# Attention moved ahead by half a batch, scores of both token halves in one stay, and M's last two quarters made in the batch that uses them

## The chip, the cores and the metric

The kernel runs on one core of a Trainium2 chip. The metric is the device time of one execution in microseconds (us), here the median of three runs. The profile shows one further execution, instruction by instruction, on the five engines: TensorE (PE, with its weight loads as PEld), VectorE (DVE), ScalarE (ACT), GpSimd (POOL) and SyncE (SP), which issues almost all DMAs.

## The reference, cut to what matters

There are 8 batches of 576 tokens and 8 heads of 64. Thirty-two packed queries `p` attend to `k` and `v`; then all tokens `q` attend to the 32 packed rows. The result goes through a two-layer MoE expert with a gate.

```
def sm_attn(qq, kk, vv):
    s = scale * np.matmul(qq, kk.transpose(0, 1, 3, 2))
    s = s - np.max(s, axis=-1, keepdims=True)
    a = np.exp(s)
    a = a / (np.sum(a, axis=-1, keepdims=True) + 1e-09)
    return np.matmul(a, vv)
p_packed = sm_attn(p, k, v)
out = sm_attn(q, p_packed, p_packed)          # B, H, S, D
x = out.transpose(0, 2, 1, 3).reshape(B * S, H * D)
h = x @ w_in                                   # 512 -> 2048
g = h * np.clip(h + 3.0, 0.0, 6.0) / 6.0
return g @ w_out                               # 2048 -> 512
```

## The kernel before

**What is multiplied.** `out @ w_in` is not formed as such. For each batch the kernel makes M = (packed rows) x `w_in` in four column quarters (`u_m`, L528) and multiplies the second attention's probabilities `a` with it. Each fp32 value is split into a high and a low part (`hi`, `lo`), so each product is three fp32r matmuls. The first product of a step, `ps_hh<-a,m` (L929), is six matmuls; the gate follows (ACT L940, then DVE L941), and the second product goes into accumulators `acc` (L969).

**Steps.** From batch 1 on, a batch is two halves of tokens (c = 0 and c = 1), each with 16 steps over the 16 column blocks f of `w_in`. The document counts steps 0 to 31 within a batch as s = 16 c + position. In batch 1, c = 0, every block is a step of `moe` (L1014). All later halves run `moe_pairs` (L1106): twelve steps form six pairs (four pairs in batch 1) whose second product is a seven-product scheme on half tiles with prepared combinations T1, T2, T4 of `w_out` (tiles `wt`), and the last four steps are single. Products go into four PSUM accumulators A, B, C and D; C and D are free between a half's last pair and the next half's first pair, except that in odd batches the edge rows use D at the end of c = 0. A pair's product is issued one to two steps after its blocks were gated.

**Combinations.** `combine(i)` (L1057) makes pair i's combinations in batch 1 at the steps listed in `TURN`: POOL adds (L1071), DVE subtracts (L1082 to L1095), and `kept` (L1073) splits each of four results with an ACT cast (L1075) and a DVE subtraction (L1076). Pairs 0, 1 and 4, 5 share two slots, are stored in DRAM and fetched back by `fetch_t` (L1103) at the steps in `FETCHES`.

**Attention of the next batch** runs in between, a few pieces at each step. `fill` (L1401) advances generators; `STAGES` gives for each the step at which it starts and how many pieces it makes per step. `attention_inputs` (L558) loads `p`, `k` and the first `q` tiles and turns them with DVE transposes (L322, L555); `attention` (L579) holds `u_s1` (scores of the packed queries, maximum, exponential), the turns of `q`, `u_ets` (transposes of the exponentials, L440 and L447), `u_pvs` (product with `v`, L470, scaled on DVE at L474) and `u_ppt` (L480, L482); `u_s2` makes the second scores and `u_a` the probabilities (DVE L502 to L524). A load's buffer, `nat`, exists twice and is shared with the upper `v` rows.

**Stays.** Scores, M and the product with `v` use small tiles of the array (64 x 32 and the like) while all else uses 128 x 128. A run of such small matmuls on PE is called a stay. `both_halves` (L362) makes the scores of the two token halves in one stay or in two; in one stay it needs two more PSUM banks, which `spare_ps` (L325) takes from C and D.

**M's quarters.** `first_quarters` (L1382) fetches three quarters of `w_in` in turn into one buffer (`w_again`, shared with `v_nat`) from s = 21 of the batch before, makes M from each, finishes all three at s = 31 and then fetches the fourth, which `late` makes in the first steps of the batch itself.

**What sets the order.** Each engine runs its instructions in order. Within what the code above allows, a scheduler places them; `behind_gates` (L542) and `issue_after` keep attention work behind the gate of the step before. SP's queue, too, is in order: a load that waits for a buffer holds up all later ones.

Of the kernel before, what the change touches and what calls it, by code (L numbers as in the profile page):

```python
# [19 lines left out]

STAGES = (((0, 1), (6, 2), (19, 2)), ((0, 1), (10, 2), (19, 1)))


LATE = (3, 2, 1, 2, 1)
PAIRS = 6
FIRST_PAIRS = 4
TURN = (
    (5, 5, 6, 6, 7, 7, 7), (7, 8, 8, 9, 9, 9, 10), (10, 10, 11, 11, 12, 12, 12), (13, 13, 13, 14, 14, 15, 15),  # L30
    (27, 27, 28, 28, 28, 29, 29), (29, 29, 30, 30, 30, 31, 31),
)
FETCHES = (((5, 1), (7, 0)), ((5, 4), (7, 5)))

# [41 lines left out]
def packed_attention_moe(  # L78
# [150 lines left out]
                yield  # L229

    def att_ps():
        return spare_ps(0) if steady else ps_a.tile([P, 512], F32, name="ps1", tag="att")

    def att_pair():

# [138 lines left out]
    def u_s1(b):  # L374
        kt = [state.pop(("k", b, a)) for a in range(NPAIR)]
        pt = state.pop(("p", b))
        e = [ap.tile([P, NST * P], F32, name="e", tag="e", bufs=4) for _ in range(2)]
        mx = [sm.tile([P, 2], F32, name="mx") for _ in range(2)]
        for part in both_halves(b == 1, pt, kt):
            if part is None:  # L380
                yield 1
                continue
            hf, banks = part
            for x, s in enumerate(banks):
                nc.scalar.copy(out=e[x][:, hf * HS:(hf + 1) * HS], in_=s)
                yield 1
                nc.vector.reduce_max(out=mx[x][:, hf:hf + 1], in_=s, axis=AX.X)
                yield None if x else 1
        for x in range(2):
            nb = sm.tile([P, 1], F32, name="nb")  # L390
            nc.vector.tensor_scalar(
                out=nb, in0=mx[x][:, 0:1], scalar1=mx[x][:, 1:2], scalar2=-scale, op0=ALU.max, op1=ALU.mult
            )
            yield 1
            den = sm.tile([P, 1], F32, name="den")
            rinv = sm.tile([P, 1], F32, name="rinv")
            state["e", b, x] = (e[x], rinv)
            nc.scalar.activation(
                out=e[x][:, :S], in_=e[x][:, :S], func=AF.Exp, bias=nb, scale=scale, accum_out=den
            )  # L400
            yield
            nc.vector.tensor_scalar_add(den, den, 1e-9)
            yield 1
            nc.vector.reciprocal(rinv, den)
            yield 1
# [79 lines left out]
    def u_s2(b):  # L485
        qt = [state.pop(("q", b, a)) for a in range(NPAIR)]
        z = [ap.tile([P, T, NPK], F32, name="z", tag="e", bufs=4) for _ in range(2)]
        for part in both_halves(not roles, pps[b % 2], qt):
            if part is None:
                yield 1  # L490
                continue
            hf, banks = part
            for x, s in enumerate(banks):
                nc.vector.transpose(out=z[x].rearrange("p t n -> p (t n)")[:, hf * HS:(hf + 1) * HS], in_=s)
                yield None if x else 1
        for x in range(2):
            yield from u_a(b, x, z[x])
# [57 lines left out]
        nc.vector.transpose(out=t, in_=state.pop(("nat", which, b, a)))  # L555
        state[which, b, a] = t

    def attention_inputs(b):  # L558

        load_p(b)  # L560
        load("k", b, 0)
        load("k", b, 1)
        yield
        transpose_p(b)
        turn("k", b, 0)
        load("k", b, 2)
        yield
        turn("k", b, 1)
        load("k", b, 3)
        yield  # L570
        turn("k", b, 2)
        load("q", b, 0)
        yield
        turn("k", b, 3)
        load("q", b, 1)
        load_v_low(b)
        yield

    def attention(b):  # L579

        yield from coarse(u_s1(b))
        turn("q", b, 0)
        load("q", b, 2)
        yield
        turn("q", b, 1)
        load("q", b, 3)
        yield
        yield
        turn("q", b, 2)
        load_v_high(b, 0)  # L590
        yield
        turn("q", b, 3)
        load_v_high(b, 1)
        yield
        yield from coarse(u_ets(b))
        yield from coarse(u_pvs(b))
        yield
        yield from coarse(u_ppt(b))
# [458 lines left out]
    def combine(i):  # L1057

        if i == 0:
            tiles = [wr.tile([P, 4, 2, H2], F32R, name=f"wt{n}", tag=f"w_in{n}") for n in (1, 2, 3)]  # L1060
            for k, name in enumerate(("T1", "T2", "T4")):
                for pair in range(PAIRS):
                    n, at = ((0, k), (1, k), (2, k), ((2, 0, 1)[k], 3))[pair % 4]
                    blocks[pair, name] = [tiles[n][:, at, x] for x in range(2)]
            for n in range(2):
                slots[n] = tiles[n].bitcast(F32)[:, :3]
        x, y = (xp.tile([P, W + P], F32, name="wx", tag="tb")[:, :H2] for _ in range(2))

        def whole(dst, name):
            hi, lo = (z.bitcast(F32) for z in block(i, name))  # L1070
            nc.gpsimd.tensor_tensor(out=dst, in0=hi, in1=lo, op=ALU.add)  # L1071

        def kept(name, made):  # L1073
            hi, lo = block(i, name)
            nc.scalar.copy(out=hi, in_=made)  # L1075
            nc.vector.tensor_sub(out=lo, in0=made, in1=hi.bitcast(F32))  # L1076

        whole(x, "T3")
        yield
        whole(y, "B22")  # L1080
        yield
        nc.vector.tensor_sub(out=y, in0=x, in1=y)  # L1082
        hi, lo = (z.bitcast(F32) for z in block(i, "B11"))
        nc.vector.tensor_sub(out=x, in0=x, in1=hi)
        nc.vector.tensor_sub(out=x, in0=x, in1=lo)
        yield
        kept("T1", x)
        yield
        nc.vector.tensor_sub(out=x, in0=hi, in1=y)
        nc.vector.tensor_add(out=x, in0=x, in1=lo)  # L1090
        kept("T2", x)
        yield
        hi, lo = (z.bitcast(F32) for z in block(i, "B21"))
        nc.vector.tensor_sub(out=x, in0=hi, in1=x)
        nc.vector.tensor_add(out=x, in0=x, in1=lo)  # L1095
        kept("T4", x)
        yield
        kept("T3", y)
        if i % 4 < 2:
            nc.sync.dma_start(out=t_kept[i % 4 + i // 4 * 2], in_=slots[i % 4].rearrange("p a x m -> p (a x m)"))  # L1100
        yield
# [4 lines left out]
    def moe_pairs(b, c, fill):  # L1106

        pairs = list(range(FIRST_PAIRS if b == 1 else PAIRS))
        if c == 0:
            pairs.reverse()  # L1110
        n_pairs = len(pairs)
        steps = [2 * i + k for i in pairs for k in range(2)] + list(range(2 * n_pairs, NF))

# [265 lines left out]
        t = w_in_sb[n] = wr.tile([P, FPC, NPAIR, P], F32, name="w_again", tag="w_in0")  # L1379
        nc.sync.dma_start(out=t.rearrange("p f a e -> p (f a e)"), in_=w_kept[n])  # L1380

    def first_quarters(b):  # L1382

        for n in range(NCH - 2, -1, -1):
            fetch_w_in(n)
            yield
            yield
            yield from coarse(u_m(b, n))

    for b in range(1, B):  # L1390
        more = b + 1 < B
        inputs, packed, ahead = (x(b + 1) if more else iter(()) for x in (attention_inputs, attention, u_s2))
        ahead = coarse(ahead)
        if b == 1:
            late = coarse(part for n in range(1, NCH) for part in u_m(1, n))
            turned = [combine(i) for i in range(PAIRS)]
        else:
            late = coarse(u_m(b, NCH - 1))
        soon = first_quarters(b + 1) if more else iter(())

        def fill(c, f):  # L1401
            s = c * NF + f
            with behind_gates():
                if b == 1:
                    for _ in range(LATE[s] if s < len(LATE) else 0):
                        next(late, None)
                    if s == 0:
                        with tc.issue_after(state["stored"].ins):
                            for n in range(NCH):
                                keep_w_in(n)  # L1410
                    for i in range(PAIRS):
                        for _ in range(TURN[i].count(s)):
                            next(turned[i], None)
                else:
                    if s > 0:
                        next(late, None)
                    for at, i in FETCHES[c]:
                        if f == at:
                            fetch_t(i)
                if s >= 21:  # L1420
                    next(soon, None)
                if s == 31 and more:
                    rest(soon)
                    fetch_w_in(NCH - 1)
            with tc.issue_after(state["load"].ins), behind_gates():
                for chain, (start, count) in zip((inputs, packed, ahead), STAGES[b > 1]):
                    for _ in range(count if s >= start else 0):
                        next(chain, None)

        for c in range(2):  # L1430
# [3 lines left out]
                roles.extend((3, 0, 1, 2))  # L1434
            else:
                moe_pairs(b, c, lambda f, c=c: fill(c, f))
        if b == 1:
            rest(*turned)
    with tc.manual_schedule(engines={mybir.EngineType.PE}):
        second(0)  # L1440

# [28 lines left out]
```

## Time and profile before

| | us |
|---|---|
| median of 3 runs | 714.29 |
| the three runs | 712.60, 714.29, 716.05 |
| the profiled execution | 714.18 |
| its span, first to last instruction | 712.39 |

| part of the span (time of first products) | from, us | length, us |
|---|---|---|
| start and batch 0 | 0 | 117.8 |
| batch 1, c = 0 | 117.8 | 51.0 |
| batch 1, c = 1 | 168.8 | 43.5 |
| batch 2 | 212.3 | 80.3 |
| batch 3 | 292.6 | 88.9 |
| batch 4 | 381.5 | 77.6 |
| batch 5 | 459.1 | 89.1 |
| batch 6 | 548.2 | 77.6 |
| batch 7 to the end | 625.8 | 86.6 |

The profile names an instruction by engine, line, output and inputs. A row that groups instructions gives their count, busy time, mean duration in ns, and the idle time of the engine before them. Busy time of PE counts a matmul's whole way through the array; several overlap, so a distance from start to start says more of its pace than a duration.

### The profile page before, as it was taken

To read this page: it belongs to the slowest core of one execution; us is meant where nothing else is said; L and a number is where in the kernel's file an instruction comes from. 1 tells how busy PE (TensorE), PEld (TensorE's weight loads), DVE (VectorE), ACT (ScalarE), POOL (GpSimd) and SP (SyncE) were. 2 spreads that over 40 slices of the span, in tenths; PEclk is the share of its full clock that TensorE was granted. 3 is DMA by queue.
4 is the path that set the end of the run, shared out by engine and by line. 5 is a ranking of instruction groups with operands and counts; after the bars stand their busy time and mean duration, and the time that the engine had idled before them with its cause. 6 is when DMAs were issued, how large, how long until landed. Compare 5 with 4: busy or idle time off the path is not lost.

```text
span 712.4 us, 16083 instructions
## 1 busy us (share of the span) xinstructions
PE 689.5 (97%) x5906; PEld 592.2 (83%) x5906; DVE 533.8 (75%) x1164; ACT 429.1 (60%) x1015; POOL 349.1 (49%) x542
## 2 busy tenths in 40 slices
PE   6599999999999999999999999999999999999997
PEld 4477877777877988899798998889888998889997
DVE  2897788688999769886598867887488877975453
ACT  5788976455565655566366655657366664756353
POOL 2565532444443454465453544556354445547453
PEclk9699999999999999999999999999999999999999
DMA  9999842955237756374554656375543845331020
GB/s 278 302 240 239 218 116 110 268 147 126 103 112 188 171 140 213 112 175 80 126 201 131 160 125 212 119 153 133 127 164 119 169 119 178 120 136 44 31 104 29
DMA packets 199102, 107.48 MB, mean 151 GB/s; under 512 B 173424, under 2 KB 185200, under 8 KB 195440
## 3 DMA queue, kind: packets, MB, share of 16 engines
q1 hardware_dynamic: 198480, 106.26, 54.4%
q8 instruction: 46, 0.75, 0.5%
q14 instruction: 32, 0.26, 0.1%
q10 hardware_dynamic: 544, 0.20, 0.1%
HBM read 89.65 MB, written 16.78 MB: 149 GB/s over the span
## 4 chain that ended last, share of the span: by engine, by line
PE 82%; DVE 10%; DMA 3%; ACT 2%; issue 1%; POOL 1%; SPq 1%; DVEq 0%; ACTq 0%
PE acc L969 47%; PE ps_hh L929 22%; PE ps L350 6%; PE ps_h L607 3%; PE ps L470 1%; DMA nat<-in_k_dram 1%; DVE tr L555 1%; DVE wt L1076 1%; PE ps L440 1%; DVE t L941 1%; SPq L294 1%; DMA w_again<-w_kept 1%; DMA k_nat<-in_k_dram 1%; ACT wt L1075 1%; PE ps L273 1%
## 5 line engine op out<-in xcount | busy, mean ns | idle before, releaser
L929 PE MATMUL ps_hh<-a_hi,m_hi 128*128 128x320 f32 (+1 forms) x448 | 133.9, 299 | 0.9 <-DVE tb L941 0.4
L929 PE MATMUL ps_hh<-a_lo,m_hi 128*128 128x320 f32 (+1 forms) x448 | 133.4, 298 | 0.0
L929 PE MATMUL ps_hh<-a_hi,m_lo 128*128 128x320 f32 (+1 forms) x448 | 132.8, 296 | 0.0
L941 DVE SCALAR_TENSOR_TENSOR t<-t,ps_hh 128x320 f32<-128x320 f32 (+1 forms) x148 | 66.0, 446 | 63.9 <-ACT t L940 63.3
L947 POOL TENSOR_TENSOR gf<-tb,gf 128x256 fp32r<-128x256 f32 x76 | 63.9, 841 | 86.9 <-ACT gf L946 49.3
L969 PE MATMUL acc<-wo_hi,g 128*128 128x512 f32 x288 | 103.2, 401 | 0.0
L940 ACT ACTIVATE t<-ps_hh,three 128x320 f32<-128x320 f32 (+1 forms) x148 | 73.6, 500 | 35.2 <-PE ps_hh L929 29.1
L929 PEld LDWEIGHTS ps_hh<-a_hi,m_hi 128*128 128x128 f32 x448 | 84.6, 189 | 9.1 <-DVE t L941 2.7
L929 PEld LDWEIGHTS ps_hh<-a_lo,m_hi 128*128 128x128 f32 x448 | 84.7, 189 | 6.4 <-issue 3.5
L929 PEld LDWEIGHTS ps_hh<-a_hi,m_lo 128*128 128x128 f32 x448 | 84.6, 189 | 2.8 <-issue 2.5
L947 POOL TENSOR_TENSOR g<-t,g 128x256 fp32r<-128x256 f32 x72 | 54.8, 762 | 45.2 <-ACT g L946 24.1
L969 PE MATMUL acc<-wt,ga 128*128 128x256 f32 x456 | 74.6, 284 | 0.2 <-ACT ga L946 0.2
L969 PE MATMUL acc<-wo_hi,ge 128*128 128x256 f32 x304 | 71.7, 286 | 1.4 <-ACT ge L946 0.8
L947 POOL TENSOR_TENSOR ga<-t,ga 128x256 fp32r<-128x256 f32 x76 | 62.4, 822 | 13.7 <-ACT ga L946 12.4
L969 PEld LDWEIGHTS acc<-wt,ga 128*128 128x128 f32 x456 | 63.1, 190 | 3.2 <-ACT gf L946 1.4
L969 PEld LDWEIGHTS acc<-wo_hi,g 128*128 128x128 f32 x288 | 53.1, 189 | 13.0 <-POOL g L947 3.4
L969 PEld LDWEIGHTS acc<-wo_hi,ge 128*128 128x128 f32 x304 | 53.0, 190 | 9.9 <-DVE t L941 2.5
L965 POOL COPY bnd<-t 128x64 f32<-128x64 f32 x76 | 22.3, 293 | 71.8 <-DVE t L941 68.1
L969 PE MATMUL acc<-wo_lo,g 128*128 128x512 f32 x144 | 57.1, 396 | 0.0
L555 DVE STREAM_TRANSPOSE tr<-nat 128x576 f32<-128x576 f32 x56 | 42.3, 763 | 17.5 <-DMA nat<-in_q_dram 10.9
L946 ACT CAST g<-t 128x256 fp32r<-128x256 f32 x72 | 29.2, 407 | 33.3 <-DVE t L941 32.8
L947 POOL TENSOR_TENSOR edge<-bnd,edge 128x256 fp32r<-128x256 f32 (+1 forms) x50 | 32.7, 659 | 33.1 <-ACT edge L946 33.1
(218 smaller groups left out, 1844.9 us busy)
## 6 DMA issues: line engine op xcount, KB each, us to landing
w_again<-w_kept SPq DMA_DIRECT2D x24, 1024.0 KB, 4.9
wt<-t_kept SPq DMA_DIRECT2D x24, 768.0 KB, 5.3
out_dram<-osb SPq DMA_DIRECT2D x33, 256.0 KB, 2.6
nat<-in_k_dram SPq DMA_DIRECT2D x112, 72.0 KB, 3.3
nat<-in_q_dram SPq DMA_DIRECT2D x112, 72.0 KB, 2.6
raw_out<-in_moe_w_out_dram SPq DMA_DIRECT2D x10, 512.0 KB, 4.8
raw_in<-in_moe_w_in_dram SPq DMA_DIRECT2D x10, 512.0 KB, 5.0
w_kept<-w_in_sb SPq DMA_DIRECT2D x4, 1024.0 KB, 7.5
```

Of the source, the lines that this page charges most:

```text
L273: nc.tensor.matmul(banks[x][NPK * a:NPK * a + NPK, :n * P], state["pp"][half, NPAIR * x + a], cols[half, :, a], start=True, stop=True,)
L294: nc.sync.dma_start(out=t[r:r + 32], in_=src[b, 2 * a + h, :, 32 * c:32 * c + 32].rearrange("(t i) j -> i t j", i=32),)
L350: nc.tensor.matmul(pair[x][NPK * a:NPK * a + NPK, :n], rows[half, a], c, start=True, stop=True)
L555: nc.vector.transpose(out=t, in_=state.pop(("nat", which, b, a)))
L607: nc.tensor.matmul(h[:, hf, :HS], mm[:, g, fs], aa[:, hf * HS:(hf + 1) * HS], start=(g == 0 and i == 0), stop=(g == NG - 1 and i == 2),)
L929: state["first"] = nc.tensor.matmul(h[:, :n], mm[:, g, fs], aa[:, t0:t0 + n], start=(g == 0 and i == 0), stop=(g == NG - 1 and i == 2),)
L940: state["relu"] = nc.scalar.activation(out=t[:, :n], in_=h, func=AF.Relu, bias=three)
L941: state["gate"] = nc.vector.scalar_tensor_tensor(out=t[:, :n], in0=t[:, :n], scalar=6.0, in1=h, op0=ALU.min, op1=ALU.mult)
L946: nc.scalar.copy(out=hi, in_=x)
L947: engine.tensor_sub(out=lo, in0=x, in1=hi.bitcast(F32))
L965: nc.gpsimd.tensor_copy(out=bnd[:, f, side * REM:side * REM + REM], in_=t[:, boff:boff + REM])
L969: nc.tensor.matmul(out, lhs[x], rhs[y], start=first and i == 0, stop=last and i == 2, skip_group_check=True)
```

## The change

The scheme is the same, and each engine has nearly the same instructions; they stand elsewhere.

- `attention_inputs` and `attention` become `keys` (loads and turns of `p`, `k`, the loads of the first two `q` tiles), the scores `u_s1`, and `values` (the rest). `keys(b + 2)` now runs in c = 1 of batch b, `u_s1(b + 2)` in its last two steps, `values(b + 1)` from the first step of batch b on, and `u_s2(b + 1)` from s = 16 (even b) or 13 (odd b) instead of 19. Batches 1 and 2 have starts of their own.
- Both token halves in one stay: `u_s1` of batches 4 to 7 and `u_s2` of batches 3, 5 and 7.
- `att_ps` takes a bank of the attention's own pair of banks instead of C's or D's.
- `quarters` makes M's quarters 2 and 1 in the batch before, and 0 and 3 in the batch that uses them; nothing is flushed at s = 31.
- The combinations of pairs 4 and 5 start a step earlier, and their `lo` subtractions (eight) go from DVE to POOL. In batch 2, c = 0, the order of pairs is 3, 4, 5, 2, 1, 0, and pairs 0 and 1 are fetched at positions 7 and 9.

```
-STAGES = (((0, 1), (6, 2), (19, 2)), ((0, 1), (10, 2), (19, 1)))
+STAGES = (((0, 1), (6, 2), (19, 2), (22, 1), (30, 3)), ((0, 1), (0, 1), (16, 1), (17, 1), (30, 3)))
+ODD = 13
...
-    (27, 27, 28, 28, 28, 29, 29), (29, 29, 30, 30, 30, 31, 31),
+    (26, 26, 27, 27, 27, 28, 28), (28, 29, 29, 30, 30, 31, 31),
...
+LATE_FETCHES = ((7, 0), (9, 1))
...
     def att_ps():
-        return spare_ps(0) if steady else ps_a.tile([P, 512], F32, name="ps1", tag="att")
+        return att_pair()[0] if steady else ps_a.tile([P, 512], F32, name="ps1", tag="att")
...
-        for part in both_halves(b == 1, pt, kt):
+        for part in both_halves(b == 1 or b > 3, pt, kt):
...
-        for part in both_halves(not roles, pps[b % 2], qt):
+        for part in both_halves(b == 1 or (b > 2 and b % 2 == 1), pps[b % 2], qt):
...
-            nc.scalar.copy(out=hi, in_=made)
-            nc.vector.tensor_sub(out=lo, in0=made, in1=hi.bitcast(F32))
+            split(hi, lo, made, nc.gpsimd if i >= FIRST_PAIRS else nc.vector)
...
-            pairs.reverse()
+            pairs = [3, 4, 5, 2, 1, 0] if b == 2 else pairs[::-1]
...
-        for n in range(NCH - 2, -1, -1):
+        for n in (2, 1, 0, 3):
             fetch_w_in(n)
             yield
             yield
             yield from coarse(u_m(b, n))
...
+        late, soon = soon, quarters(b + 1) if b + 1 < B else iter(())
+        chains = [
+            keys(2) if b == 1 else coarse(u_s1(3)) if b == 2 else iter(()),
+            values(b + 1) if b + 1 < B else iter(()),
+            coarse(u_s2(b + 1)) if b + 1 < B else iter(()),
+            keys(b + 2) if b + 2 < B else iter(()),
+            coarse(u_s1(b + 2)) if 1 < b < B - 2 else iter(()),
+        ]
+        stages = [list(x) for x in STAGES[b > 1]]
+        if b > 1 and b % 2:
+            stages[2][0] = ODD
+        elif b == 2:
+            stages[:2] = (0, 1), (3, 1)
...
-                if s == 31 and more:
-                    rest(soon)
-                    fetch_w_in(NCH - 1)
```

Three places show how this moves instructions. The first is PE in batch 1 around s = 17 and 18, where `pn` (the product with `v`, scaled by DVE) is transposed for the second scores. Before, this transpose (L480) stood inside a second product (`acc`), ahead of the first product of s = 18:

```order
L969 MATMUL acc<-wo_hi,g_2269 128x512
L969 MATMUL acc<-wo_lo,g_2269 128x512
L969 MATMUL acc<-wo_hi,g_2269 128x512 x2
L480 MATMUL ps_x<-ident,pn 128x128
L969 MATMUL acc<-wo_lo,g_2269 128x512
L969 MATMUL acc<-wo_hi,g_2269 128x512
```

Now the product with `v` itself stands inside that second product, and the transpose (L482) comes after the first products of s = 18 and s = 19, of which these are the last three matmuls, and ahead of the first pair's product:

```order
L934 MATMUL ps_hh<-a_hi,m_hi 128x256
L934 MATMUL ps_hh<-a_lo,m_hi 128x256
L934 MATMUL ps_hh<-a_hi,m_lo 128x256
L482 MATMUL ps_2195<-ident,pn 128x128
L974 MATMUL acc<-wo_hi,gf 128x256
L974 MATMUL acc<-wo_lo,gf 128x256
```

So the transpose has moved behind twelve first-product matmuls and the rest of that second product.

The second place is PE at the scores of the packed queries with the keys. Before, batch 4 made those of batch 5 for one token half between a first product and a pair's product, and for the other in a stay of its own further on (the same row, with output `ps_5724`):

```order
L929 MATMUL ps_hh<-a_hi,m_lo 128x256
L350 MATMUL ps_5708<-tr,p_tr 32x288 x8
L969 MATMUL acc<-wo_hi,gf 128x256
L969 MATMUL acc<-wo_lo,gf 128x256
L969 MATMUL acc<-wo_hi,gf 128x256
```

Now both sets of eight stand side by side; these are batch 5's scores at the change from batch 3 to batch 4 (`ps_x` are C and D):

```order
L974 MATMUL acc<-wo_lo,g_5388 128x512
L352 MATMUL ps_x<-tr,p_tr 32x288 x8
L352 MATMUL ps_5343<-tr,p_tr 32x288 x8
L974 MATMUL acc<-wo_hi,g_5388 128x512 x2
L934 MATMUL ps_hh<-a_hi,m_hi 128x256
```

The later set has moved up to the earlier one, and there are seven such joined sets, four of `p_tr` and three of `pps`.

The third place is DVE in batch 4 from s = 16, the first step of c = 1, to the gate of s = 18 (`SCALAR_TENSOR_TENSOR t<-t,ps_hh`). Before:

```order
L941 SCALAR_TENSOR_TENSOR t<-t,ps_hh 128x320
L1196 TENSOR_TENSOR t<-t 128x128
L947 TENSOR_TENSOR ge<-t,ge 128x256
L941 SCALAR_TENSOR_TENSOR tb<-tb,ps_hh 128x320
L1204 TENSOR_TENSOR t<-t,tb 128x2x128
L1209 TENSOR_TENSOR tb<-tb,t 128x128
L474 TENSOR_SCALAR pn<-ps_5946,rinv 128x64 x2
L1167 SCALAR_TENSOR_TENSOR osb<-acc,osb 128x512 x2
L941 SCALAR_TENSOR_TENSOR t<-t,ps_hh 128x320
```

Now, from the last of four transposes of scores (`z`) ahead of the gate of s = 17 to the gate of s = 18:

```order
L496 STREAM_TRANSPOSE z<-ps_x 128x288
L946 SCALAR_TENSOR_TENSOR tb<-tb,ps_hh 128x320
L1171 SCALAR_TENSOR_TENSOR osb<-acc,osb 128x512
L1208 TENSOR_TENSOR t<-t,tb 128x2x128
L1171 SCALAR_TENSOR_TENSOR osb<-acc,osb 128x512
L1213 TENSOR_TENSOR tb<-tb,t 128x128
L504 TENSOR_REDUCE mx_6085<-z 128x18
L324 STREAM_TRANSPOSE p_tr<-p_nat 128x128
L557 STREAM_TRANSPOSE tr<-nat 128x576
L946 SCALAR_TENSOR_TENSOR t<-t,ps_hh 128x320
```

The scores of `u_s2`, the turns of `p` and `k` and their loads now fall together in the first steps of c = 1.

More of the change, by code (lines that the diff above doesn't have):

```diff
@@ L556, in turn, with keys @@
         state[which, b, a] = t
-    def attention_inputs(b):
+    def keys(b):
         load_p(b)
@@ L575, in attention_inputs, with values @@
         load("q", b, 1)
-        load_v_low(b)
         yield
[L579 to L594, printed above, removed]
-        yield from coarse(u_ets(b))
+    def values(b):
+        if b == 2:
+            load_v_low(b)
+            yield from coarse(u_s1(b))
+        for a in range(2):
+            turn("q", b, a)
+            load("q", b, a + 2)
+            yield
+        if b == 2:
+            yield
+        for a in range(2):
+            turn("q", b, a + 2)
+            load_v_high(b, a)
+            yield
+        yield from coarse(u_ets(b))
+        if b > 2:
+            yield
+            load_v_low(b)
+            yield
+            yield
         yield from coarse(u_pvs(b))
@@ L1380, in fetch_w_in, with quarters @@
         nc.sync.dma_start(out=t.rearrange("p f a e -> p (f a e)"), in_=w_kept[n])
-    def first_quarters(b):
-        for n in range(NCH - 2, -1, -1):
+    def quarters(b):
+        for n in (2, 1, 0, 3):
             fetch_w_in(n)
@@ L1388, in first_quarters @@
             yield from coarse(u_m(b, n))
+    soon = coarse(part for n in range(1, NCH) for part in u_m(1, n))
+    turned = [combine(i) for i in range(PAIRS)]
     for b in range(1, B):
[L1391 to L1399, printed above, removed]
+        late, soon = soon, quarters(b + 1) if b + 1 < B else iter(())
[11 more added lines that the diff above has]
+            stages[:2] = (0, 1), (3, 1)
         def fill(c, f):
@@ L1410, in fill @@
                                 keep_w_in(n)
-                    for i in range(PAIRS):
-                        for _ in range(TURN[i].count(s)):
-                            next(turned[i], None)
-                else:
-                    if s > 0:
-                        next(late, None)
-                    for at, i in FETCHES[c]:
+                else:
+                    next(late, None)
+                    for at, i in LATE_FETCHES if (b, c) == (2, 0) else FETCHES[c]:
                         if f == at:
                             fetch_t(i)
+                for i in range(PAIRS if b == 1 else 0):
+                    for _ in range(TURN[i].count(s)):
+                        next(turned[i], None)
                 if s >= 21:
                     next(soon, None)
-                if s == 31 and more:
-                    rest(soon)
-                    fetch_w_in(NCH - 1)
             with tc.issue_after(state["load"].ins), behind_gates():
-                for chain, (start, count) in zip((inputs, packed, ahead), STAGES[b > 1]):
+                for chain, (start, count) in zip(chains, stages):
                     for _ in range(count if s >= start else 0):
@@ L1436, in packed_attention_moe @@
                 moe_pairs(b, c, lambda f, c=c: fill(c, f))
-        if b == 1:
-            rest(*turned)
     with tc.manual_schedule(engines={mybir.EngineType.PE}):
```

## The prediction

> **What bounds the kernel now.** I read the page first, then the busy times by stretch, then PE's waits, and then single instructions at those waits.
>
> ```profile
> span 712.4 us, 16083 instructions
> PE 689.5 (97%) x5906; PEld 592.2 (83%) x5906; DVE 533.8 (75%) x1164; ACT 429.1 (60%) x1015; POOL 349.1 (49%) x542
> ```
> ```profile
> 0.00:155.00 155.00, 140.72 (x1185) 109.55 (x1186) 114.00 (x233) 110.63 (x219) 72.89 (x88) 0.96 0.78 212
> 155.00:235.00 80.00, 75.79 (x627) 61.38 (x626) 71.01 (x154) 46.14 (x118) 35.54 (x52) 1.00 0.52 140
> 235.00:680.00 445.00, 444.87 (x3890) 394.80 (x3891) 333.20 (x745) 256.97 (x641) 225.42 (x381) 1.00 0.50 137
> 680.00:712.00 32.00, 28.10 (x209) 26.50 (x207) 15.59 (x34) 15.35 (x39) 15.26 (x23) 1.00 0.21 74
> ```
>
> In the second view the columns after the stretch are PE, PEld, DVE, ACT and POOL busy. PE is the bound. From 235 to 680 us it is idle for 0.13 us of 445, so there the change can gain only by taking work from PE. The 14.3 us idle before 155 us lie almost all in the start, whose plan is untouched, and the last 3.9 us are the tail of batch 7, whose second half has the same order as before. What waiting there is to remove lies from 155 to 235 us, in batch 1 and the start of batch 2: 80.00 - 75.79 = 4.2 us. PE's waits there:
>
> ```profile
> PE ps_x L480 <- DVE pn L474: 1.4, 1, 1.4
> PE acc L969 <- ACT ga L946: 0.8, 2, 0.6
> PE acc L969 <- ACT ge L946: 0.8, 2, 0.6
> PE ps_hh L929 <- DVE tb L941: 0.4, 1, 0.4
> PE ps_hh L929 <- DVE t L941: 0.3, 1, 0.3
> ```
>
> DVE is busy for 71.0 of these 80 us. The ACT casts waited for are themselves behind DVE's gate work, so all of these waits come from a late DVE. The sum below is made against the profiled execution: 714.18 us, span 712.39, 1.8 us around it. It stands 0.11 us below the median of 714.29.
>
> **Fewer stays.** No matmul is added or left out. What PE saves is the change of array tiling around a stay:
>
> ```profile
> 479.86 0.31 PE L929 MATMUL ps_hh<-a_lo,m_hi 128*128 128x320 f32 x1
> 480.01 0.31 PE L929 MATMUL ps_hh<-a_hi,m_lo 128*128 128x320 f32 x1
> 480.25 0.71 PE L350 MATMUL ps<-tr,p_tr 64*32 64x288 f32 x16
> 480.89 0.39 PE L969 MATMUL acc<-wo_hi,gf 128*128 128x256 f32 x1
> 481.11 0.28 PE L969 MATMUL acc<-wo_lo,gf 128*128 128x256 f32 x1
> 481.23 0.28 PE L969 MATMUL acc<-wo_hi,gf 128*128 128x256 f32 x1
> ```
>
> The pace of 320-column matmuls is 0.15 us from start to start; the last before the stay takes 0.24, so going in costs 0.09. The first after it takes 0.22 where the next takes 0.12, so coming out costs 0.10. Seven stays vanish (four `u_s1`, three `u_s2`): 7 x 0.19 = **-1.3 us**. This is certain as long as C and D are read out before the next half's first pair needs them. At s = 30 they have three steps for that. At s = 16 the pair follows after s = 18, and in the order DVE reads them out before the gate of s = 17. I cost it at nothing; if DVE is late by more than a step there, it appears as a backlog, which is counted below.
>
> **The wait for `pn`.** PE's longest wait, and what DVE did in it:
>
> ```profile
> 172.10 0.62 PE L969 MATMUL acc<-wo_hi,g 128*128 128x512 f32 x2
> 174.15 0.33 PE L480 MATMUL ps_x<-ident,pn 128*128 128x128 f32 x1 [1.43 <-DVE pn L474]
> ```
> ```profile
> 171.05 0.84 DVE L1090 TENSOR_TENSOR wx<-wx,wo_lo 128x256 f32<-128x256 f32 x1
> 172.37 0.42 DVE L1076 TENSOR_TENSOR wt<-wx,wt 128x256 fp32r<-128x256 f32 x1 [0.47 <-ACT wt L1075]
> ...
> 173.63 0.47 DVE L474 TENSOR_SCALAR pn<-ps,rinv 128x64 f32<-128x64 f32 x2
> ```
>
> DVE works through the combinations of pair 3, and `pn` stands behind them. In the changed order the product with `v` comes about two steps later, behind the combinations on DVE, and the transpose two first products (2 x 6 x 0.12 us) and nine further matmuls after it. That is over 3 us of PE work as cover against 0.47 us of DVE work. The wait goes: **-1.4 us**. What is late next is `u_s2`, whose first scores follow a step later; PE has a whole pair's product in between. Bounds: 0 (the wait moves on) to -1.4.
>
> **The backlog of batch 1.** Of the remaining 2.8 us of waits, 27.30 - 26.39 + 16.70 - 15.49 = 2.1 us lie in two stretches, the end of batch 1 and the first steps of batch 2:
>
> ```profile
> 185.00:212.30 27.30, 26.39 (x194) 20.50 (x193) 26.05 (x51) 16.16 (x40) 13.31 (x18) 1.00 0.29 106
> 212.30:229.00 16.70, 15.49 (x115) 12.99 (x114) 16.36 (x38) 9.51 (x26) 5.19 (x8) 1.00 0.75 201
> ```
>
> DVE is busy for 26.05 of 27.3 us and then for 16.36 of 16.7, so here its amount of work counts. From s = 19 of batch 1 to s = 7 of batch 2 the change takes off DVE the eight `kept` subtractions and one quarter of M (two subtractions), and puts on three turns of `q`, four maxima of `u_s1(3)` and some seven small operations (about 0.17 us each):
>
> ```profile
> L1076 DVE TENSOR_TENSOR wt<-wx,wt 128x256 fp32r<-128x256 f32 x12 | 5.6, 464 | 1.8 <-ACT wt L1075 1.4
> ```
> ```profile
> L539 DVE TENSOR_TENSOR m_lo<-ps,m_hi 128x512 fp32r<-128x512 f32 x40 | 27.4, 684 | 6.2 <-ACT m_hi L537 6.0
> L555 DVE STREAM_TRANSPOSE tr<-nat 128x576 f32<-128x576 f32 x36 | 27.1, 763 | 12.8 <-DMA nat<-in_q_dram 10.4 <-DMA nat<-in_k_dram 2.2
> L509 DVE TENSOR_REDUCE den<-z 128x18 f32<-128x576 f32 x10 | 7.4, 741 | 0.0
> L515 DVE TENSOR_TENSOR z<-z,den 128x576 f32<-128x576 f32 x10 | 8.6, 860 | 0.2
> L387 DVE TENSOR_REDUCE mx<-ps 128x1 f32<-128x288 f32 x20 | 8.9, 444 | 3.4 <-ACT e L385 3.4
> L1209 DVE TENSOR_TENSOR tb<-tb,t 128x128 f32<-128x128 f32 x58 | 34.6, 597 | 1.0
> L1196 DVE TENSOR_TENSOR t<-t 128x128 f32<-128x128 f32 x59 | 18.8, 319 | 1.5
> ```
>
> Off: 8 x 0.464 + 2 x 0.684 = 5.1 us. On: 3 x 0.763 + 4 x 0.444 + 1.2 = 5.3 us. The relief that the moved subtractions bring is used up by the attention that moves in, so I take **0** for this term, between -2.8 (all these waits go) and +1.5 (each result of pairs 4 and 5 now waits for POOL, too).
>
> **What the earlier attention puts on DVE in c = 1.** From s = 16 to s = 25 of batch 4, and likewise of batch 2:
>
> ```profile
> 417.40:443.50 26.10, 26.10 (x286) 22.83 (x286) 19.18 (x46) 14.82 (x35) 13.11 (x23) 1.00 0.65 193
> 421.43 1.30 PE ps L470 x80
> ```
>
> DVE has 6.9 us left of 26.1. Moving in are four turns of `k` (3.05), `p`'s (0.3), a sum (0.74), a product (0.86) and a reciprocal (0.26); moving out are `pn` and a copy of `pps` (0.85). That is 4.4 us of durations, about 3.9 once the overlap of some 0.07 us between consecutive instructions is taken off. Meanwhile PE loses the product with `v` (1.30 us, the row from the chain) and about 1 us of other stays. So DVE would have 23.1 us of work in some 23.7 us of PE's time. It fits by the sum, but DVE also waits for casts, exponentials and loads, and cannot use all of it. I estimate 0.6 us of new waits in each of batches 2 and 4, and none in batch 6, which turns no keys: **+1.2 us**. Bounds: 0, as in all of 235 to 680 us now, and 2 us each, about the waits of the end of batch 1 and the start of batch 2 together, where DVE is as full.
>
> **What it puts at the start of c = 0.** The scores' maxima and the turns of `q` now stand in s = 0 to 3 of batches 3 to 6.
>
> ```profile
> 381.50:391.00 9.50, 9.50 (x76) 8.00 (x75) 8.57 (x20) 5.60 (x14) 2.63 (x4) 1.00 0.73 214
> ```
>
> DVE is 90% busy there already, and gets 2.5 us more while PE gets about one more (the second set of scores). The steps after s = 4 have slack that absorbs the rest. I take 0.15 us for each of four starts, **+0.6 us**, between 0 and 0.6 (2.5 - 1.0 - the 0.9 that DVE had left) each.
>
> **Edits that I cost at nothing,** with what hides them. The transpose of `e`'s rest now waits for both ACT copies of its bank pair, but `u_pvs` comes two steps later (cover gone: under 0.7 us a batch, by M's equally large subtraction, 0.684). M's quarters 0 and 3 are needed at s = 8 and s = 12 and are made at about s = 3 and s = 9. SP's fetch of quarter 3 now stands behind eight loads of upper `v` rows, and these behind the turns of `q` at s = 2 and 3.
>
> ```profile
> w_again<-w_kept SPq DMA_DIRECT2D x24, 1024.0 KB, 4.9
> wt<-t_kept SPq DMA_DIRECT2D x24, 768.0 KB, 5.3
> nat<-in_q_dram SPq DMA_DIRECT2D x112, 72.0 KB, 2.6
> ```
> ```profile
> 551.37 1.95 SPq L294 DMA_DIRECT2D nat<-in_k_dram  x4
> ```
>
> SP takes 1.95 us to issue four loads, so about 4 us for eight; with 4.9 us to land after s = 3, quarter 3 is there by s = 7 or 8, at 2.4 us a step (batch 4's 77.6 us in the table, by 32). In batch 2 the fetch of pair 1 waits for pair 5's product and has about two steps, hardly its 5.3 us; a miss costs up to 2 us, once.
>
> **Sum:** -1.3 - 1.4 + 0 + 1.2 + 0.6 = -0.9 us, so 714.18 - 0.9 = **713.3 us**, no change that a measurement can tell: about 0.5% (3.6 us) is what it takes for this kernel. With the ends of the terms near it, this case spans 711 to 715.5 us.
>
> **The rivals.**
>
> *DVE keeps up everywhere (faster).* No new waits, and most of the 2.8 us go because DVE's work is spread better: -1.3 - 1.4 - 2.0 = -4.7, so 709.5 us, at the very best -5.5 (all 2.8). For it: from 235 to 680 us PE waits for nothing although DVE is 73% busy in the stretch above. Against it: the work sums above show no relief where it is short.
>
> *DVE becomes the bound of whole stretches (slower).* Place: c = 1 of batches 2 to 5, where `u_s2`, the turns of `k` and M's quarters fall together. A gate that is late by more than a pair's second product (21 matmuls of 0.12 = 2.5 us) stops PE, since that product is all that PE has in between. DVE's lag would be 3.9 us of work moved in and 2.4 us of cover moved out; if it passes 2.5 us in each of these four halves by 1.3 us, and the four starts wait 0.5 us each, that is 5.2 + 2.0 = 7.2 us against a gain of 2.7, so 718.7 us. It decides once the lag passes 2.5 us. For it: 97% of the time there by my sum (23.1 of 23.7).
>
> *The moved subtractions hold up DVE (a little slower).* L1209 and L1196 do the same kind of work on the same size, but L1209 runs beside POOL's subtraction of `gf` and takes 0.597 against 0.319 us. If each moved subtraction delays DVE by those 0.28 us, it is 8 x 0.28 = 2.2 us, on the path where DVE is saturated: 713.3 + 2.2 = 715.5 us. [...]
>
> *The joined stays save nothing,* because the scheduler tears the sets apart: the order shows them side by side, so I give it no chance of its own; it would be 714.6 us.
>
> **How the numbers follow.** Forecast 0.40, DVE keeps up 0.35, DVE bound 0.18, subtractions 0.07. The range reaches from 708.0 (the best case is 708.7) to 719.0, past the slower case. Faster by over 0.5% (under 710.7 us): 0.35. Slower by over 0.5% (over 717.9 us): the DVE case and a part of the next, 0.20. Within: 0.45.
>
> **What would show it.** The wait of the transpose for `pn` gone from PE's waits; sixteen score matmuls in one piece at seven places; PE's idle time from 155 to 235 us at about 2.8 us, and new waits of about half a us at s = 22 to 27 of batches 2 and 4. Wrong would be the forecast if PE stays free of waits after 235 us and those of batch 1 halve, or if PE's waits on DVE there come to several us per batch.

## The result, and the profile after

| | us |
|---|---|
| the kernel before, median of 9 runs | 714.14 (712.60 to 716.05) |
| the changed kernel, median of 9 runs | 718.34 (717.10 to 719.84) |
| ratio | 1.0063, 95% interval 1.0047 to 1.0078 |
| the same, measured again beside the last experiments | 719.74, ratio 1.0072 (1.0059 to 1.0086) |

The change makes the kernel slower by 4.2 us, a little more than the 0.5% that a measurement can tell. The forecast was no change (713.3). The time lies inside the range and close to that of the slower rival (718.7), though not by that rival's account.

The page of the changed kernel begins:

```profile
span 717.1 us, 16105 instructions
PE 690.4 (96%) x5906; PEld 594.9 (83%) x5906; DVE 518.4 (72%) x1156; ACT 428.5 (60%) x1015; POOL 358.3 (50%) x550
```

PE's busy time is nearly what it was (+0.9 us); the other 3.8 us of span are idle time. The busy times by stretch say where (columns as before: length, PE, PEld, DVE, ACT, POOL, PE's granted clock, DMA share, GB/s). First the changed kernel:

```profile
155.00:235.00 80.00, 77.99 (x667) 64.90 (x666) 71.11 (x165) 50.38 (x128) 43.50 (x60) 1.00 0.60 158
235.00:300.00 65.00, 59.87 (x542) 52.41 (x542) 45.03 (x101) 32.72 (x80) 29.39 (x51) 1.00 0.53 135
300.00:680.00 380.00, 378.68 (x3290) 337.36 (x3289) 273.20 (x629) 217.99 (x547) 195.24 (x326) 1.00 0.46 134
```

and the kernel before, in the second of these stretches:

```profile
235.00:300.00 65.00, 65.00 (x592) 56.45 (x593) 51.57 (x118) 38.33 (x93) 30.79 (x55) 1.00 0.57 157
```

From 155 to 235 us PE's idle time has halved, from 4.2 to 2.0 us. From 235 to 300 us, which is batch 2 but for its first steps, PE was never idle and now is for 5.1 us of 65. From 300 to 680 us it is idle for 1.3 us, where it was for 0.1. So most of the loss lies in one batch. PE's waits there (line waited for; total, times, longest), from 230 to 300 us:

```profile
PE acc L974 <- DVE z L496: 1.9, 2, 1.1
PE acc L974 <- DMA wt<-t_kept: 1.9, 1, 1.9
PE acc L974 <- ACT ga L951: 0.7, 1, 0.7
PE ps_hh L934 <- DVE tb L946: 0.6, 1, 0.6
```

One of them is for a transfer. In PE's timeline (start, duration, last the idle time before and what ended it), with SP's queue beside it:

```profile
238.93 0.60 PE L442 MATMUL ps<-ident,e 128*128 128x128 f32 x4
241.45 0.63 PE L974 MATMUL acc<-wt,gf 128*128 128x256 f32 x3 [1.92 <-DMA wt<-t_kept]
```
```profile
235.29 0.41 SPq L1108 DMA_DIRECT2D wt<-t_kept  x1
235.74 2.97 SPq L421 DMA_DIRECT2D v_nat<-in_v_dram  x3
238.76 1.26 SPq L411 DMA_DIRECT2D v_nat<-in_v_dram  x2
249.66 4.95 SPq L296 DMA_DIRECT2D nat<-in_k_dram  x8
254.70 0.44 SPq L1384 DMA_DIRECT2D w_again<-w_kept  x1
255.24 1.80 SPq L316 DMA_DIRECT2D p_nat<-in_p_dram  x4
```

This is the fetch of pair 1 into the slot that pair 5 had just left: issued at 235.29, landed 6.1 us later and used at 241.45. The same rows show the second cause. SP issues nothing from 240.0 to 249.66 us, and its own waits name the reason:

```profile
SPq L296 <- PE ps L472: 9.9, 1, 9.9
```

The key loads of batch 4 wait until PE's product with `v` (L472) has read the buffers that they share with the upper `v` rows. Behind them in SP's order stand a quarter of `w_in` (1 MB) and then `p` of batch 4, issued at 255.24. DVE in the meantime:

```profile
258.52 0.47 DVE L946 SCALAR_TENSOR_TENSOR t<-t,ps_hh 128x320 f32<-128x320 f32 x1
261.34 0.31 DVE L324 STREAM_TRANSPOSE p_tr<-p_nat 128x128 f32<-128x128 f32 x1 [2.34 <-DMA p_nat<-in_p_dram]
261.57 0.44 DVE L496 STREAM_TRANSPOSE z<-ps_x 128x288 f32<-128x288 f32 x1
261.94 0.74 DVE L557 STREAM_TRANSPOSE tr<-nat 128x576 f32<-128x576 f32 x1
```

DVE stands still for 2.34 us before the turn of `p`, with the transposes of the second scores (`z`), the turns of `k` and the next gates queued behind it, and from there it works without a gap until past 280 us. PE's two waits for `z` are that backlog: the next pair's products need the accumulators C and D, and these still hold the joined scores (`ps_x`) that DVE's `z` transposes have yet to read. The waits for `ga` and `tb` come later in the same half; e1 shows that they stand without the gap, too.

Where the time went, stage by stage, for two profiles of each kernel. The numbers are sums over PE's rows: the distance from one matmul's start to the next, less the usual distance between two of these kinds, where that is over 0.13 us (so a little more than the idle times). "Again" is a second profile, e9 for the kernel before and e10 for the changed kernel.

| us late on PE | before | before, again | changed | changed, again | forecast of the difference |
|---|---|---|---|---|---|
| batch 1, to 208 us | 4.3 | 3.4 | 1.0 | 1.6 | -1.4 |
| first steps of batch 2, to 235 us | 1.9 | 1.7 | 1.8 | 1.8 | 0, with the rest of batch 1 |
| batch 2, the fetch of pair 1 | 0 | 0 | 2.2 | 1.8 | 0 |
| batch 2, c = 1 | 0 | 0 | 4.0 | 4.8 | +0.6 |
| batches 3 to 6 | 0.3 | 0 | 2.3 | 1.9 | +1.2 |
| tail | 0.8 | 0.8 | 0.8 | 0.8 | 0 |
| first product of batch 1 starts at | 117.8 | 120.3 | 119.0 | 119.0 | |
| from there to the end | 594.6 | 592.9 | 598.1 | 599.0 | -0.9 |

The start alone scatters by 2.5 us between executions of the same kernel, so traces are compared from the first product of batch 1 on. The stays, by the same starts, give PE back 1.8 us. So, for the first profile of each: waits 12.10 - 7.23 = +4.9, stays -1.8, and +0.5 left over in gaps of under 0.13 us, together 598.11 - 594.56 = +3.6.

### The profile page after: what moved, and what is told of

The parts are those of the page before. It is cut to its first block, busy times and chain, and to the rows that moved or that the text cites. A ratio compares the mean times of both kernels' runs of the same rounds, so it can differ in the third digit from the quotient of the medians.

```text
span 717.1 us, 16105 instructions
## 1 busy us (share of the span) xinstructions
PE 690.4 (96%) x5906; PEld 594.9 (83%) x5906; DVE 518.4 (72%) x1156; ACT 428.5 (60%) x1015; POOL 358.3 (50%) x550
## 4 chain that ended last, share of the span: by engine, by line
PE 74%; DVE 13%; DMA 4%; issue 2%; ACT 2%; POOL 2%; SPq 1%; DVEq 0%; POOLq 0%; ACTq 0%
PE acc L974 42%; PE ps_hh L934 20%; PE ps L352 4%; PE ps_h L612 3%; DVE tr L557 2%; DMA nat<-in_k_dram 1%; PE ps L472 1%; DMA wt<-t_kept 1%; SPq L296 1%; DVE t L946 1%; DMA nat<-in_q_dram 1%; PE ps_t L683 1%; DVE mx L504 1%; DVE osb L1171 1%; PE ps L442 1%
## 5 line engine op out<-in xcount | busy, mean ns | idle before, releaser
L951 ACT CAST ge<-t 128x256 fp32r<-128x256 f32 x76 | 30.7, 404 | 32.1 <-DVE t L1200 31.9
L974 PE MATMUL acc<-wt,gf 128*128 128x256 f32 x228 | 47.5, 283 | 1.9 <-DMA wt<-t_kept 1.9
L945 ACT ACTIVATE tb<-ps_hh,three 128x256 f32<-128x256 f32 (+1 forms) x76 | 38.0, 500 | 19.1 <-PE ps_hh L934 16.8
L970 POOL COPY bnd<-t 128x64 f32<-128x64 f32 x76 | 24.8, 327 | 48.6 <-DVE t L946 47.3
```

Source lines behind the costliest of these rows:

```text
L945: state["relu"] = nc.scalar.activation(out=t[:, :n], in_=h, func=AF.Relu, bias=three)
L951: nc.scalar.copy(out=hi, in_=x)
L970: nc.gpsimd.tensor_copy(out=bnd[:, f, side * REM:side * REM + REM], in_=t[:, boff:boff + REM])
L974: nc.tensor.matmul(out, lhs[x], rhs[y], start=first and i == 0, stop=last and i == 2, skip_group_check=True)
```

## The experiments

Theory A: two late transfers in batch 2 make the loss, pair 1's fetch directly and `p` of batch 4 by way of DVE. Theory B: DVE has too much work in c = 1, whatever arrives late. Unless said otherwise the edits are made to the changed kernel; ratios are to the kernel before, run on the same chip beside them.

**e1: turn `p` of batch 4 later.**

```
-        transpose_p(b)
+        transpose_p(b) if b != 4 else None
...
-        turn("k", b, 1)
+        turn("k", b, 1), transpose_p(b) if b == 4 else None
```

> Only the turn of p for batch 4 moves, behind two turns of k and one transpose of scores on DVE, so that 2.3 us of other DVE work stands ahead of it; loads and all else as in the changed kernel. Theory A (the late load of p holds up DVE for 2.34 us in c=1 of batch 2 and the backlog never clears): DVE's wait for p_nat goes, PE's waits in c=1 of batch 2 fall from 4.0 us to about 0.8 (what batch 4 has there with the same work), time 718.3 - 3.2 = 715.1. Theory B (DVE has too much work there whatever comes late): the waits stay above 3 us, time 717.3 to 718.5.

716.79 us, ratio 1.0035 (1.0023 to 1.0047). DVE's timeline:

```profile
259.77 0.48 DVE L946 SCALAR_TENSOR_TENSOR t<-t,ps_hh 128x320 f32<-128x320 f32 x1
260.17 0.47 DVE L496 STREAM_TRANSPOSE z<-ps_x 128x288 f32<-128x288 f32 x1
260.57 0.73 DVE L557 STREAM_TRANSPOSE tr<-nat 128x576 f32<-128x576 f32 x1
261.23 0.24 DVE L1200 TENSOR_TENSOR t<-t 128x128 f32<-128x128 f32 x1
261.40 0.76 DVE L557 STREAM_TRANSPOSE tr<-nat 128x576 f32<-128x576 f32 x1
262.12 0.31 DVE L324 STREAM_TRANSPOSE p_tr<-p_nat 128x128 f32<-128x128 f32 x1
```

The same load, the same work, and no gap: PE's two waits for `z` (1.9 us in the waits above) are gone. Two others of that half stay at their size:

```profile
PE acc L974 <- ACT ga L951: 0.7, 1, 0.7
PE ps_hh L934 <- DVE tb L946: 0.6, 1, 0.6
```

In start-to-start sums c = 1 of batch 2 falls from 4.0 to 1.7 us, so the 2.34 us for which DVE stood still had reached PE almost one for one. It does not fall to 0.8: both theories hold a part. The time fell by less than theory A said (716.79, not 715.1). The rest of the expected gain went elsewhere in this execution. PE's wait for pair 1's fetch was longer, and its clock behind it was halved (a stretch, and PE's timeline):

```profile
242.00:245.00 3.00, 3.00 (x16) 3.00 (x15) 0.00 (x0) 0.00 (x0) 0.00 (x0) 0.50 0.01 2
```
```profile
241.21 0.62 PE L974 MATMUL acc<-wt,gf 128*128 128x256 f32 x3 [2.29 <-DMA wt<-t_kept]
241.67 1.40 PE L974 MATMUL acc<-wt,ga 128*128 128x256 f32 x6
242.87 0.41 PE L974 MATMUL acc<-wo_hi,ge 128*128 128x256 f32 x1
243.08 0.41 PE L974 MATMUL acc<-wo_lo,ge 128*128 128x256 f32 x1
```

At a granted clock of 0.50, matmuls start 0.21 us apart instead of 0.12; some 17 of them cost 1.5 us more. That is this one execution; it does not say why the median fell by so little.

**e2: pair 0 ahead of pair 1 in batch 2.**

```
-            pairs = [3, 4, 5, 2, 1, 0] if b == 2 else pairs[::-1]
+            pairs = [3, 4, 5, 2, 0, 1] if b == 2 else pairs[::-1]
```

> In batch 2, c=0, pair 0 is used before pair 1; the fetches stay where they are. If the wait of 1.9 us is only pair 1's fetch being too young when its product comes (issued at 235.3, landed at 241.4 us, six microseconds after pair 5 freed its slot), pair 0's product covers it: the wait goes, nothing else moves, 718.3 - 1.9 = 716.4. If the queue is late as a whole, the wait moves to pair 0 or stays: 718.3. The wait for p in c=1 stays in both cases, since it hangs on PE's product with v.

716.73 us, ratio 1.0031 (1.0019 to 1.0043). PE has no wait at all from 230 to 250 us: pair 0's product covers pair 1's fetch. c = 1 stays as bad as it was (4.6 us). As expected.

**e3: both edits.**

> Both edits together. If the two waits of batch 2 are separate and are what the forecast lacked, the savings add: 718.3 - 1.9 - 3.2 = 713.2, about 0.9 below the kernel before, which was the forecast for the change. If c=1 of batch 2 is short of DVE time anyway: 716 or more.

715.02 us, ratio 1.0005 (0.9995 to 1.0015): level with the kernel before. The two together are 0.0058 of the ratio, some 4 us, and make up nearly the whole loss. But 713.2 was not reached. With PE 2 us earlier, `p` is late again, now by 0.73 us:

```profile
259.81 0.31 DVE L324 STREAM_TRANSPOSE p_tr<-p_nat 128x128 f32<-128x128 f32 x1 [0.73 <-DMA p_nat<-in_p_dram]
```

A turn of `k` follows late by 0.65 us, and PE has 3.1 us of late starts in c = 1.

**e4: the moved subtractions back on DVE.**

```
-            split(hi, lo, made, nc.gpsimd if i >= FIRST_PAIRS else nc.vector)
+            split(hi, lo, made, nc.vector)
```

> The eight subtractions of pairs 4 and 5 go back from POOL to DVE. Theory 'relief': DVE gets 8 x 0.43 = 3.4 us more in the stretch where it is saturated, and PE's waits from 185 us to s=7 of batch 2 rise by 1 to 3 us: 719.3 to 721. [...]

717.17 us, ratio 1.0038 (1.0026 to 1.0050). The time is below the 719.3 to 721 of the theory 'relief' and 1.2 us below the changed kernel, as if the subtractions cost more on POOL. But the gain is not at the place in question: from 185 to 235 us PE is late by 0.7 us more, while the wait for pair 1's fetch falls from 2.2 to 0.9 us and c = 1 of batch 2 from 4.0 to 2.9. The edit had also shifted the order of instructions, on PE too, at the end of batch 1, so the gain need not come from the subtractions; e8 asks again.

**e8: e3 with the subtractions back on DVE.**

> e3 with the eight subtractions back on DVE. In e4 that gained 1.2 us, of which 1.3 is a shorter wait for the fetch of pair 1 by its trace, and nothing at the subtractions' own place (their stretch has 0.7 us more of waits). With e3 the fetch is covered already. If the fetch was the gain: 715.0 + 0.7 = 715.7. If POOL holding up DVE was the cost: 713.7.

715.51 us, ratio 1.0018 (1.0007 to 1.0029), against e3's 1.0005. PE's waits from 185 to 235 us, first e3, then e8:

```profile
PE ps_hh L934 <- DVE tb L946: 0.8, 1, 0.8
PE ps_hh L934 <- DVE t L946: 0.7, 2, 0.3
PE acc L974 <- POOL ga L952: 0.2, 1, 0.2
```
```profile
PE ps_hh L934 <- DVE tb L946: 1.0, 1, 1.0
PE acc L974 <- ACT ga L951: 0.8, 1, 0.8
PE ps_hh L934 <- DVE t L946: 0.6, 2, 0.3
```

With the fetch covered, the gain of e4 is gone, and by these waits (1.7 against 2.4 us) about 0.7 us is lost: the subtractions are no worse off on POOL, and by the traces a little better. The two ratios alone do not settle it, since their intervals overlap.

**e5: stays apart again.**

```
-        for part in both_halves(b == 1 or b > 3, pt, kt):
+        for part in both_halves(b == 1, pt, kt):
...
-        for part in both_halves(b == 1 or (b > 2 and b % 2 == 1), pps[b % 2], qt):
+        for part in both_halves(b == 1, pps[b % 2], qt):
```

> The changed kernel with the seven joined stays taken apart again (u_s1 of batches 4 to 7 and u_s2 of batches 3, 5 and 7 in two stays each). Term 1 of the prediction (0.19 us each): seven more entries and exits, PE loses 1.3 us to them, time 718.3 + 1.3 = 719.6; PE's own rows in the changed kernel say up to 1.8. Rival: the joined sets ask for C and D and give DVE eight reads at once, and that costs as much as the stays save: time within 0.5 of 718.3 or below it, with PE's waits lower by over a microsecond.

722.74 us, ratio 1.0126 (1.0105 to 1.0147): 4.4 us above the changed kernel, over three times the term. PE's starts show what it is made of: 1.7 us are entries, exits and the stays themselves, and most of the rest is new late starts (15.7 against 12.1 us). One of them, 1.2 us, is PE waiting for DVE's `z` ahead of a second set of scores. That the others come from the same cause, the second set a step later and DVE's work behind it, is likely but was not tested. This profile also has 3 us at a clock of 0.50, after a wait of 1.90 us, so its own span overstates the loss.

**e6: load `p` early instead of turning it late** (with e2's order).

```
-        load_p(b)
+        load_p(b) if b != 4 else None
...
-            load_v_low(b)
+            load_v_low(b), load_p(4) if b == 3 else None
```

> As e3's order of pairs, but instead of turning p of batch 4 later its load is issued half a batch earlier, so that neither its turn nor anything behind it waits for it. Theory A (what is left in c=1 of batch 2 hangs on late loads: e3 still shows 0.73 us of DVE waiting for p and 0.65 for k): PE's waits in c=1 of batch 2 fall from 3.1 us to about 1, time 715.0 - 2 = 713. Theory B (DVE is short of time there): they stay at 2.5 us or more, time 714.5 to 715.5.

715.61 us, ratio 1.0019 (1.0007 to 1.0030). PE's waits from 230 to 300 us:

```profile
PE ps L352 <- DMA w_again<-w_kept: 1.7, 1, 1.7
PE acc L974 <- DVE ge L952: 0.5, 1, 0.5
PE ps_hh L934 <- DVE t L946: 0.2, 1, 0.2
```

The waits on DVE fall from 3.1 to 1.0 us, as theory A said, but the time does not fall with them: PE now gets to M's next quarter before its fetch has landed (issued at 274.1, landed at 282.2 us) and waits 1.7 us there. The edit also moved more than the load: the scaling of `pn` stands four gates later on DVE than in e3, and the first `z` at 260.6 instead of 257.1 us. So the fall of the waits on DVE is not the early load's alone.

**e7: the second scores of even batches back at s = 19, in two stays** (on e3).

```
-        for part in both_halves(b == 1 or (b > 2 and b % 2 == 1), pps[b % 2], qt):
+        for part in both_halves(b == 1, pps[b % 2], qt):
...
+        elif b > 1:
+            stages[2][0] = 19
```

> e3 with the second scores of the even batches (u_s2 of batches 3, 5 and 7) back at s=19 and in two stays, as in the kernel before; all else stays ahead. Term 4 (DVE's work in the first steps of c=1): the waits of c=1 go, 3.1 us in batch 2 and 0.8 in batch 4, against 3 x 0.25 us for the stays: 715.0 - 3.1 = 711.9. If the loads are the cause, the waits of batch 4 go and those of batch 2 halve: 713.5. If it is the turns of k and M's quarters alone: 715 to 716.

716.50 us, ratio 1.0040 (1.0026 to 1.0055), just above the last and slowest of the three cases. c = 1 of batch 2 improves from 3.1 to 1.3 us of late starts, so the early scores have a part in them. But batch 4 goes from 0.8 to 1.2, PE waits a further 0.4 us in batch 2 and 0.7 in batch 4 for a quarter of M (`w_again`), and the stays cost 0.7. From the first product of batch 1 the profile is 0.8 us longer than e3's. On balance, having the scores early in c = 1 is not what costs the time.

**e11: keys at s = 19 instead of 17** (on e6).

```
-... (16, 1), (17, 1), (30, 3)))
+... (16, 1), (19, 1), (30, 3)))
```

> e6 (p loaded early) with the keys of the batch after next started at s=19 instead of 17, so that their turns on DVE (3 us) and their loads leave the first steps of c=1. If DVE's work there (u_s2 and the turns together) makes the waits of 0.8 us in batch 4 and 0.6 to 1.0 us in batches 3 and 5, these go: 715.6 - 2 = 713.6. If it is only the total that counts, the waits move a few steps on: within 0.7 of 715.6. If the keys and the loads behind them come too late for u_s1 at s=30: above 716.5.

718.14 us, ratio 1.0050 (1.0035 to 1.0066), as slow as the last case expected, but not for its reason. The late starts do not go, they move a few steps on and grow: in batch 2 from 2.8 us (with the 1.7 above) to 4.4, in batch 4 from 0.8 to 1.5, in batch 5 from 0.6 to 1.2. PE's waits from 260 to 285 us hang on DVE and on casts behind it, and on no scores of s = 30:

```profile
PE acc L974 <- ACT gf L951: 1.5, 1, 1.5
PE acc L974 <- DVE ge L952: 0.9, 1, 0.9
PE acc L974 <- POOL gf L952: 0.3, 1, 0.3
```

At 285.8 us PE also waits 1.0 us for a quarter of M, whose fetch stands behind the loads that moved. This fits the reading that the total of DVE's work in c = 1 counts and, pushed later, meets M's quarters; but that reading gave 715.6 within 0.7, so it is not shown.

**e12: e3 with the turn of `p` behind the third key turn.**

> e3 with the turn of p one key turn further back on DVE, behind the third. e3's DVE still waits 0.73 us for p, and 0.65 for k a little later; PE waits 0.8 and 0.6 us behind them. If the wait for p makes PE's, 0.8 to 1.3 us go: 715.0 - 1 = 714.0. If the wait only moves to k: 715.0.

714.38 us, ratio 0.9997 (0.9986 to 1.0008). DVE no longer waits for `p`, PE's late starts in c = 1 fall from 3.1 to 2.3 us, and the time is level with e3's within the intervals. From the first product of s = 16 to that of s = 26 of batch 2, in e12 and then in the kernel before:

```profile
248.74:276.03 27.29, 25.97 (x207) 22.24 (x205) 23.50 (x50) 13.78 (x34) 12.16 (x22) 1.00 0.84 207
```
```profile
250.97:277.08 26.11, 26.11 (x287) 22.84 (x286) 18.90 (x44) 14.36 (x34) 13.00 (x24) 1.00 0.65 190
```

DVE is busy for 23.5 us there, where it had been for 18.9. It is fullest from 255 to 281 us: busy for 24.9 us of 26, and waiting for two loads of `k` in the other 1.1. So what is left of PE's waits is DVE's work and these two loads; no run separates them.

**e9 and e10: the two kernels once more.**

> The kernel before once more, for its profile. In the profiles so far the first product of batch 1 starts at 117.8 us in the kernel before, and between 117.5 and 119.5 in the changed kernel and the eight variants of it, though batch 0 is the same. If that is scatter of the start, it comes anywhere from 117.5 to 119.5 here, and the part from there to the end is again 594.6 us. If the changed kernels start later for a reason, it is 117.8 again.

> The changed kernel once more, for its profile and for a time beside these variants: 718.3. The part from the first product of batch 1 to the end should be 598.1 us again, with the waits of 1.9 us (fetch of pair 1) and 4.0 us (c=1 of batch 2) at the same places.

e9 took 714.98 us with the first product of batch 1 at 120.3 us, so the start scatters, a little wider than expected, and the rest came out at 592.9 us, not 594.6 (1.3 us less waiting, most of it in batch 1). e10 took 719.74 us (its ratio stands in the first table), started at 119.0 as before, and shows both waits again at the same places: 1.3 us of idle time for the fetch, 4.8 us of late starts in c = 1 of batch 2.

No version beat the kernel before: e12 and e3 are level with it.

## Why the prediction was wrong, step by step

- **Edits at nothing: the fetch of pair 1.** This step failed. The text saw that the fetch had "about two steps, hardly its 5.3 us" and priced a miss at up to 2 us, but left it out of the sum. It took 6.1 us and cost 1.9 us of idle time, and e2, which only covers it, is 1.6 us faster by the medians. A miss held likely by its own numbers belonged in the sum.
- **c = 1 of batches 2 and 4, +0.6 each.** For batch 4 this was right (0.8). For batch 2 this step failed too, and it is the larger of the two: it was 4.0, twice the bound of 2. DVE's work was summed somewhat high (for batch 4, 23.1 us in 23.7 of PE's time; measured 21.8 in 24.4), but of the loads the step only said that DVE "also waits" for them. It never followed them to where they are issued: the key loads wait for PE's product with `v`, and `p` waits behind them and behind 1 MB. 2.3 of the 4.0 us are this hole in DVE's work (e1); the rest fits the fullness that the step spoke of, with late loads of `k` in it (e12), and is not separated further.
- **Fewer stays, -1.3.** Right in kind, somewhat small: -1.8. The term had entry and exit (0.19); a joined set is also shorter than two. PE's timeline of the changed kernel:

```profile
257.07 0.31 PE L934 MATMUL ps_hh<-a_hi,m_lo 128*128 128x320 f32 x1
257.31 0.71 PE L352 MATMUL ps_x<-tr,pps 64*32 64x288 f32 x16
257.81 0.69 PE L352 MATMUL ps<-tr,pps 64*32 64x288 f32 x16
258.44 0.41 PE L934 MATMUL ps_hh<-a_hi,m_hi 128*128 128x320 f32 x1
```

  Both sets take 258.44 - 257.31 = 1.13 us from the first start to that of the matmul behind them, where one alone had taken 480.89 - 480.25 = 0.64. That would make 0.19 + 2 x 0.64 - 1.13 = 0.34 us each by these rows; over all of PE's starts it is 0.26. What this term costed at nothing failed in batch 2: with DVE late, C and D were not read out when the pair needed them, and that is how the hole in DVE's work reached PE (the two waits for `z`, 1.9 us).
- **The wait for `pn`, -1.4.** It went. In its place PE waits 0.3 us ahead of the product with `v` (L472, for a copy on DVE).
- **The backlog of batch 1, 0.** Too low in batch 1 itself: 4.3 and 3.4 us before and 1.0 and 1.6 now, so about 0.4 to 1.9 us more went than the wait for `pn`; by e8's trace up to 0.7 of it may be the subtractions on POOL. In the first steps of batch 2 it was right: about 1.8 before and after.
- **Starts of c = 0, +0.6.** They cost nothing but for 0.3 us in batch 6. Instead c = 1 of batches 3 and 5, costed at nothing, has 0.6 us each. For batches 3 to 6 together the forecast had +1.2 and the profiles show about +1.9.
- **The rival "DVE becomes the bound"** gave 718.7 and the time was 718.3, but by chance: it wanted 1.3 us in each of four halves from work alone; it was 4.0 in one half, begun by a load, plus the fetch. The rival of the moved subtractions is refuted as a cost on balance by e8: it gave 713.7 there, and 715.51 was measured. "The best case", DVE keeping up everywhere, failed mainly in batch 2; batches 3 to 6 add about 1.9 us.

Not settled: e1's median fell by less than its waits did, and how many executions run at half clock after the fetch's wait was not measured; and what keeps e3, e6 and e12 at 714.4 to 715.6, apart from DVE's fullness in c = 1 and the waits shown, was not taken apart further.

## What to carry to other kernels

When code that loads and uses data moves ahead, follow each load back to the queue that issues it: what stands ahead of it there, and whose buffer the one ahead is waiting for. Here a load for which DVE stood still for 2.34 us cost the bound engine 2.3, because its first user stood early in the order of an engine that had no time to spare behind it; putting the user a few instructions later (one line in e1) can hide it, and so can using another pair first (one digit in e2). A miss that one's own numbers make likely goes into the sum, not into a list of things that cost nothing.

## What the runs showed of the hardware

In two executions a wait of about 2 us on PE cost 1.7 to 1.8 times its length. After 1.90 us of idle time in e5 and 2.29 us in e1 the granted clock was 0.50 for over 3 us, which costs some 1.5 us; after 1.92 us in the changed kernel it stayed at 1.00. By the clock of the microseconds at both ends (0.88 and 0.92 in e1, 0.99 and 0.81 in e5) I estimate 3.4 us at half clock in both: three full microseconds, and (0.12 + 0.08) / 0.50 and (0.01 + 0.19) / 0.50 us beside them. Why the clock fell after the wait of 1.90 us and not after that of 1.92 us, no run shows.

A POOL subtraction of pairs 4 and 5 did slow DVE beside it. POOL and DVE in the changed kernel:

```profile
218.66 0.74 POOL L952 TENSOR_TENSOR wt<-wx,wt 128x256 fp32r<-128x256 f32 x1 [1.85 <-ACT wt L951]
```
```profile
218.75 0.80 DVE L1213 TENSOR_TENSOR tb<-tb,t 128x128 f32<-128x128 f32 x1
```

The same instruction while POOL does nothing:

```profile
232.80 0.28 DVE L1213 TENSOR_TENSOR tb<-tb,t 128x128 f32<-128x128 f32 x1
```

It takes 0.80 us beside the subtraction and 0.28 alone. POOL began first, and DVE's instruction ended only behind it (219.55 against 219.40 us). Of the eight subtractions two held up a DVE instruction in this way, by about half a microsecond each (the other is L1200 at 222.87 us, 0.81 us). Most other DVE instructions beside them read PSUM and took 0.38 to 0.45 us (0.68 to 0.69 us for 128x512); the means of the same groups from 235 to 640 us are 0.41 to 0.45 us (0.68 to 0.69 us).
